# First MLP of an attention + MLP + MLP kernel: relu and square in the PSUM bank of h, the high half made by ScalarE

## The chip, the cores and the metric

One core of a Trainium2 chip runs the whole program. The metric is the device time of one execution in microseconds (us), lower is better. The engines are named as in the profile: PE (TensorE, matmuls), PEld (its weight loads), DVE (VectorE), ACT (ScalarE), POOL (GpSimd) and SP (SyncE, which issues the DMAs).

## What is computed

The reference, cut to what matters (4 batches, 8 heads, 576 queries of 64 columns; 2304 tokens, 512 columns, 2048 hidden columns):

```python
scores = scale * q @ k.T + (cum[:, None] - cum[None, :])   # cum: cumulated logs of f
attn = softmax(causal(scores));  x = attn @ v               # then (2304, 512)
h = x @ w_in;  r = maximum(h, 0);  g = s * (r * r) + b      # first MLP
x = g @ w_out
h = x @ w_in2; g = maximum(0.01 * h, h); out = g @ w_out2   # second MLP
```

The weights come as float64. Matmuls run on float32 values cut into a high and a low half; a product of two such numbers is three matmuls (high·high, high·low, low·high).

## The kernel before, in words

The tokens are cut into nine units of 256 queries. Units 0 to 7 are half a batch each; the last one, here called unit 8, has the 64 queries left over in every batch. While the first MLP of a unit runs, the attention of the next one is computed between its matmuls, on all engines.

The first MLP of a unit has 16 steps, i = 0 to 15, one for each 128 hidden columns. Step i has three parts. `mlp1_h` (L688) is 12 matmuls of 256 columns into a PSUM bank, h(i); there are two such banks (`ps_h`), and four from unit 7 on. `mlp1_g` makes g(i) = relu(h)² as a high and a low half in SBUF; the tile g has two buffers. `mlp1_o` (L733) is 12 matmuls that add g(i) times the weights to the unit's sums in the banks `ps_o`; the first two of them need only the high half, the third needs the low one. In the code o(i - 1) comes behind h(i) and g(i). The eviction of the sums at a unit's end is L747 (ACT) and L749 (DVE).

In `mlp1_g` of units 1 to 8 ACT reads the bank and writes relu to an SBUF tile `graw` (L711; two buffers), squares it there (L712), POOL copies it into g's high half, rounded (L713), and DVE subtracts that from `graw` to get the low half (L714). Unit 0 takes another path (L703, L704), which stays. In unit 7 two more columns of g are filled by POOL (L709, L710).

The attention of a head goes: scores on PE (L327), decay, mask and minimum on DVE (L337; POOL writes the mask into the tile `cumk`, L296, that a DMA loads), exp on ACT (L351), the two halves of the weights on ACT (L372) and DVE (L373), a transposing DMA into `p_t`, and the product with v on PE (L394); ACT and DVE add up the result (L413, L414, L428, L429). Queries and keys are split on POOL (L242, L243) and DVE (L244, L245).

Each block of float64 weights is turned into two halves by ACT (L102), DVE (L103, L104, L106), ACT (L111) and POOL (L112). The second matrix of the first MLP gets its halves in unit 1; the second MLP's blocks are made in unit 8 and in the first steps of the second MLP (L791 and L809 are its matmuls, L798 to L801 what lies between them).

The order on each engine is set when the program is built: a list scheduler places the instructions by priorities, by a cost table and by when buffers come free. On the chip each engine runs its own list strictly in that order, and waits at the first instruction whose input or buffer isn't ready.

Of the kernel before, what the change touches and what calls it, by code (L numbers as in the profile page):

```python
# [8 lines left out]
F32 = mybir.dt.float32  # L9
# [4 lines left out]
AF = mybir.ActivationFunctionType  # L14
ALU = mybir.AluOpType
AX = mybir.AxisListType

P = 128
NQ = 384
UN = 256  # L20
# [3 lines left out]
# Float32's bits under the sign are 8 times those of a float64's top word, less 896 of exponent:  # L24
# read as a float32 (whose exponent is 1/8 of that), the top word times this is that difference.
# [3 lines left out]
# A unit is 256 queries: all heads' attention, then the first MLP. The second unit of a batch attends  # L29
# for the batch's last 64 queries too, whose MLP comes with those of the other batches in a last unit.  # L30
# (batch, first query, queries, tiles of queries)
# [8 lines left out]
def attention_moe_moe_kernel(  # L40
# [42 lines left out]
    # They come as float64; the bits become float32 here, as hi + lo, both exact in float32r.  # L83
    # A block is a contraction tile's [128, 512]; raw and split blocks share the slots.
# [12 lines left out]
    def float_w(raw, out=None):  # L97
        """The bits of float32, in place of the top words or in a tile of their own."""
# [16 lines left out]
    class Weights:  # L115
        """Blocks 2i and 2i + 1 are of w_in and w_out. Those of w_out from `late` on stay float32 for a while."""
# [46 lines left out]
    heads = [(u, h) for u in range(1, NU - 1) for h in range(H)]  # L163
    # A job is a head's whole tiles of queries, the last first (the mask goes over the decays of keys
    # that earlier queries don't see), or, between two heads, both ones' half tile. A batch's first two
    # tiles go together, side by side.
# [9 lines left out]
    # A head's columns of queries: those of its half tile stand with zeros in place of the other head's.  # L176
# [12 lines left out]
    # A head's queries and keys: all of a tile's columns, or in turn one half of them.  # L189
# [6 lines left out]
    def load_heads():  # L196
        """Those whose place the heads that were split have left."""
        while n_qk[0] < len(heads) and n_qk[0] - 1 - (small(n_qk[0]) and small(n_qk[0] - 1)) < n_qk[1]:
            load_head(n_qk[0])
            n_qk[0] += 1  # L200
# [55 lines left out]
    def split_v(j, kend):  # L256
# [9 lines left out]
        # power of two at or under each column's largest magnitude, over PSCALE  # L266
# [19 lines left out]
    def st_mask(i):  # L286
        """The causal mask, over the decays."""
# [5 lines left out]
        for e in range(P // m):  # L293
            # (the second of two tiles has its keys behind the first's)
# [13 lines left out]
    def st_score(i):  # L308
# [7 lines left out]
        for r, t in enumerate(ts):  # L316
# [3 lines left out]
            for c, (k0, kw) in enumerate(parts):  # L320
# [13 lines left out]
                # Minus the scores, and their least. Of the decay, cum[query] - cum[key], the first term  # L334
                # is one to a row: the softmax is the same without it.
# [20 lines left out]
    def st_split(i):  # L356
        """Normalise; the weights as two halves, transposed by the DMA."""
# [73 lines left out]
    def last_x1():  # L431
        """The queries that the units of the batches left."""
# [43 lines left out]
    # The tensor engine has nothing else to do yet: it works in float32, adds the decay and the  # L476
    # mask, normalises and transposes.
# [20 lines left out]
    # The cumulated logs' hi and lo halves, on both halves of the partitions, then H columns with  # L498
    # -1/SCALE at a head's rows.
# [68 lines left out]
    def first_b(h):  # L568
# [11 lines left out]
        # by block of keys, then by the queries that see it  # L580
# [71 lines left out]
    def slot_target(u, i):  # L652
        """Slots of the attention that are to be emitted by then; not beyond the next unit but one's
        first pair of heads, whose x has to wait for a slot."""
        t0, t1 = (ends[v] + (AHEAD if heavy(v + 1) else LEAD) for v in (u, u + 1))
        t = t0 + ((i + 1) * (t1 - t0)) // NF
        if u + 2 < NU - 1:
            t = min(t, ends[u + 1] + (ends[u + 2] - ends[u + 1]) * 2 // H - 1)
        return t
# [4 lines left out]
    # The last unit with the attention behind it: there are banks for sums of their own.  # L664
# [32 lines left out]
    def mlp1_g(u, i, ps):  # L697
        # r^2 alone: s(r^2)W + (b 1)W is had from (r^2)W and, by two more columns in a unit, 1W.
        n = UN + 2 * (u == UB)
        if u == 0 and i >= W_FLOAT:  # L700
            # float32 products: the weights' halves come in the next unit
# [5 lines left out]
        raw = gp.tile([P, UN], F32, tag="raw", name="graw")  # L707
# [3 lines left out]
        nc.scalar.activation(raw, ps, AF.Relu)  # L711
        nc.scalar.activation(raw, raw, AF.Square)  # L712
        nc.gpsimd.tensor_scalar(g[:, 0, :UN], raw, 1.0, 0.0, ALU.mult, ALU.add)  # L713
        nc.vector.tensor_tensor(out=g[:, 1, :UN], in0=raw, in1=g[:, 0, :UN].bitcast(F32), op=ALU.subtract)  # L714
        return g[:, :, :n]

    def mlp1_po(u):
        """The unit's sums: two to a bank, a group of products together."""
# [231 lines left out]
```

## Time and profile before

| what | value |
|---|---|
| median of 3 runs | 1104.73 us (1100.14 to 1105.5) |
| span of the profiled execution | 1104.1 us |
| PE / PEld busy | 1004.9 / 884.5 us |
| DVE / ACT / POOL busy | 710.0 / 445.5 / 342.0 us |

The span runs from the first instruction of the profiled execution to its last. That execution's own time has no row apart from the span; the median lies 0.6 us above it. Busy times of the engines overlap. Units 1 to 6 take the stretch from about 143 to 599 us, unit 7 that to 642, unit 8 that to about 706, and the second MLP the rest.

### The profile page before, as it was taken

Reading aid. Unit: us, or ns where it says so; the run is one execution under the profiler, and the core shown is the slowest. Engines: PE = TensorE matmul, PEld = TensorE weight load, DVE = VectorE, ACT = ScalarE, POOL = GpSimd, SP = SyncE. Lnnn points to the kernel's source line nnn. Section 1 sums busy time; section 2 is a strip of 40 time slices with the busy share of each in tenths; the row PEclk is TensorE's granted clock in tenths of the full one; section 3 lists DMA queues with packets and bytes.
Section 4 is the critical chain, followed back from the end, with each engine's and each line's share of the span. In section 5 each row is a group of like instructions: output and inputs, shape, how many; then the busy total and the mean of one; then the engine's idle time right before and its main releaser. Section 6 shows DMA issues by size and latency. Waiting matters only on the chain.

```text
span 1104.1 us, 18869 instructions
## 1 busy us (share of the span) xinstructions
PE 1004.9 (91%) x6600; PEld 884.5 (80%) x6600; DVE 710.0 (64%) x1682; ACT 445.5 (40%) x1074; POOL 342.0 (31%) x591
## 2 busy tenths in 40 slices
PE   6876798889899988898989999899999999999998
PEld 4676687888888878787889999767888888888887
DVE  6788977776887877787765159998523533433343
ACT  4555566554555655555554235433101111111111
POOL 4344566644454444454431225433000000000000
PEclk9998989999999999999999999999999999999999
DMA  7388555469898998888874055450200010010010
GB/s 271 125 201 242 154 129 101 98 156 170 171 196 183 211 180 159 197 176 176 187 133 117 8 192 191 124 200 1 77 1 1 20 39 1 1 39 1 0 39 20
DMA packets 191791, 129.32 MB, mean 117 GB/s; under 512 B 137872, under 2 KB 167056, under 8 KB 191696
## 3 DMA queue, kind: packets, MB, share of 16 engines
q1 hardware_dynamic: 191696, 128.12, 48.2%
q8 instruction: 52, 0.85, 0.3%
q14 instruction: 43, 0.35, 0.1%
HBM read 86.58 MB, written 10.04 MB: 88 GB/s over the span
## 4 chain that ended last, share of the span: by engine, by line
PE 47%; DMA 17%; DVE 16%; issue 10%; POOL 6%; ACT 2%; SPq 1%; POOLq 0%; DVEq 0%; ACTq 0%
PE ps_o L809 16%; PE ps_h L791 15%; DMA p_t<-p_hl 7%; PE ps_o L733 6%; PE ps_h L688 6%; DMA cumk<-cumd 4%; DMA qk_raw<-in_qk 3%; DVE wt L104 2%; DVE tt L337 2%; POOL w L112 2%; DVE wt L106 1%; DVE p_hl L373 1%; DVE g L714 1%; POOL g L713 1%; PE ps_v L394 1%
## 5 line engine op out<-in xcount | busy, mean ns | idle before, releaser
L688 PE MATMUL ps_h<-x,w 128*128 128x256 f32 x1728 | 264.3, 288 | 13.2 <-POOL w L112 7.9
L733 PE MATMUL ps_o<-g,w 128*128 128x256 f32 (+1 forms) x1536 | 237.3, 292 | 16.5 <-POOL g L713 9.8
L688 PEld LDWEIGHTS ps_h<-x,w 128*128 128x128 f32 x1728 | 235.1, 194 | 17.1 <-POOL w L112 8.9
L733 PEld LDWEIGHTS ps_o<-g,w 128*128 128x128 f32 x1536 | 206.1, 193 | 27.2 <-POOL g L713 14.3
L809 PE MATMUL ps_o<-w,g 128*128 128x512 f32 x864 | 215.6, 396 | 5.2 <-DVE g L800 3.6
L791 PE MATMUL ps_h<-x,w 128*128 128x512 f32 (+1 forms) x960 | 211.0, 368 | 0.0
L809 PEld LDWEIGHTS ps_o<-w,g 128*128 128x128 f32 x864 | 159.7, 188 | 46.4 <-DVE g L800 6.3
L791 PEld LDWEIGHTS ps_h<-x,w 128*128 128x128 f32 x960 | 169.1, 188 | 32.1
L799 DVE TENSOR_TENSOR t<-ps_h,t 128x512 f32<-128x512 f32 (+1 forms) x80 | 50.8, 635 | 176.7 <-ACT t L798 176.4
L798 ACT ACTIVATE t<-ps_h 128x512 f32<-128x512 f32 (+1 forms) x80 | 44.3, 554 | 279.3 <-PE ps_h L791 279.3
L714 DVE TENSOR_TENSOR g<-graw,g 128x256 fp32r<-128x256 f32 x128 | 70.0, 549 | 66.0 <-POOL g L713 65.9
L351 ACT ACTIVATE tt<-tt,sm 128x512 f32<-128x512 f32 (+4 forms) x128 | 76.8, 600 | 88.3 <-DVE sm L337 79.3
L327 PE MATMUL ps_s<-k_st,q_st 128*128 128x288 f32 (+4 forms) x352 | 91.8, 335 | 20.3 <-DVE sm L337 10.1
L373 DVE SCALAR_TENSOR_TENSOR p_hl<-tt,sm,p_hl 128x512 f16<-128x512 f32 (+4 forms) x128 | 87.5, 692 | 22.5 <-ACT p_hl L372 21.4
L372 ACT ACTIVATE p_hl<-tt,sm 128x512 f16<-128x512 f32 (+4 forms) x128 | 73.5, 596 | 60.3 <-DMA p_t<-p_hl 46.5
L112 POOL TENSOR_TENSOR w<-wt,w 128x512 fp32r<-128x512 f32 x48 | 68.1, 1421 | 79.4 <-ACT w L111 77.8
L296 POOL TENSOR_SCALAR_AFFINE_SELECT cumk<-cumk 128x128 f32<-128x128 f32 (+2 forms) x120 | 46.9, 392 | 137.4 <-DMA cumk<-cumd 99.1
L394 PE MATMUL ps_v<-p_t,v_st 128*128 128x128 f16 (+1 forms) x912 | 60.5, 214 | 27.0 <-DMA p_t<-p_hl 23.8
L327 PEld LDWEIGHTS ps_s<-k_st,q_st 128*128 128x128 f32 x352 | 59.1, 194 | 26.6 <-DVE sm L337 15.1
L713 POOL TENSOR_SCALAR g<-graw 128x256 fp32r<-128x256 f32 x128 | 63.4, 497 | 50.7 <-ACT graw L712 41.1
L337 DVE CUSTOM_DVE_ANT_0 tt<-ps_s,cumk 128x512 f32<-128x512 f32 (+4 forms) x128 | 63.2, 497 | 23.5 <-POOL cumk L296 18.7
L394 PEld LDWEIGHTS <-v_st 128*128 128x128 f16 x912 | 46.8, 100 | 36.7 <-issue 15.8
(88 smaller groups left out, 1116.8 us busy)
## 6 DMA issues: line engine op xcount, KB each, us to landing
w_raw<-in_moe_w_in SPq DMA_DIRECT2D x32, 512.0 KB, 5.4
w_raw<-in_moe_w_out SPq DMA_DIRECT2D x32, 512.0 KB, 5.3
qk_raw<-in_qk SPq DMA_DIRECT2D x32, 480.0 KB, 4.5
cumk<-cumd SPq DMA_DIRECT2D x32, 256.0 KB, 4.3
qk_raw<-in_qk SPq DMA_DIRECT2D x24, 256.0 KB, 3.9
x1d<-x1o SPq DMA_DIRECT2D x36, 128.0 KB, 2.4
cumk<-cumd SPq DMA_DIRECT2D x32, 144.0 KB, 3.5
v_raw<-in_v SPq DMA_DIRECT2D x16, 288.0 KB, 4.2
```

Of the source, the lines that this page charges most:

```text
L112: nc.gpsimd.tensor_tensor(w[:, 1], x, w[:, 0].bitcast(F32), ALU.subtract)
L327: nc.tensor.matmul(o, q_st[j + e][:, q0 - u0 : q0 - u0 + P], k_st[j + e][:, a, k0 : k0 + kw], start=(e == 0 and a == 0), stop=(e == ne - 1 ...
L337: nc.vector.tensor_tensor_reduce(tt[:, at + k0 : at + k0 + kw], o, cumk[jb][:, at + k0 : at + k0 + kw], scale=-SCALE, scalar=3.0e38 if c = ...
L351: nc.scalar.activation(e, e, AF.Exp, bias=sm[:, r : r + 1], scale=-1.0, accum_out=sm[:, 2 + r : 3 + r])
L373: nc.vector.scalar_tensor_tensor(v[:, 1, :w], e, inv, v[:, 0, :w], ALU.mult, ALU.subtract)
L394: nc.tensor.matmul(av[:, at + e * m : at + (e + 1) * m], v_st[j + e][:, k].rearrange("p l d -> p (l d)"), pt[:, to + l * nk + k, e * m : ( ...
L688: nc.tensor.matmul(ps, wi[:, a, d * P : (d + 1) * P], x[:, c, d], start=(d == 0 and n == 0), stop=(d == ND - 1 and n == 2),)
L713: nc.gpsimd.tensor_scalar(g[:, 0, :UN], raw, 1.0, 0.0, ALU.mult, ALU.add)
L714: nc.vector.tensor_tensor(out=g[:, 1, :UN], in0=raw, in1=g[:, 0, :UN].bitcast(F32), op=ALU.subtract)
L733: nc.tensor.matmul(po[d], wo[:, a, d * P : (d + 1) * P], g[:, c], start=(first and n == 0), stop=(last and n == 2),)
L791: nc.tensor.matmul(ps[:, :n], wi[:, a, d * P : (d + 1) * P], x[:, e, d, :n], start=(d == 0 and k == 0), stop=(d == ND - 1 and k == 2),)
L809: nc.tensor.matmul(po[m], g[:, a, m * P : (m + 1) * P], wo[:, e, :], start=(i == 0 and k == 0), stop=(i == NF - 1 and k == 2),)
```

## The change

Relu and square of h now write back into the bank of h itself. ACT, in place of POOL, copies the bank into g's high half, and DVE subtracts from the bank. The tile `graw` is gone, and POOL has only the two extra columns of unit 7 left to do for g. The bank of h(i) is thus in use until the subtraction of step i has ended. Comments were also taken out of the file; as one line (the tile) is gone, lines behind it are one less in the changed kernel: relu, square, copy and subtraction are L710 to L713 there, and o(i) is L732.

```diff
         g = gp.tile([P, 2, UN + 2], F32R, tag="g", name="g", bufs=2)
-        raw = gp.tile([P, UN], F32, tag="raw", name="graw")
         if u == UB:
             nc.gpsimd.memset(g[:, 0, UN:].bitcast(F32), 1.0)
             nc.gpsimd.memset(g[:, 1, UN:].bitcast(F32), 0.0)
-        nc.scalar.activation(raw, ps, AF.Relu)
-        nc.scalar.activation(raw, raw, AF.Square)
-        nc.gpsimd.tensor_scalar(g[:, 0, :UN], raw, 1.0, 0.0, ALU.mult, ALU.add)
-        nc.vector.tensor_tensor(out=g[:, 1, :UN], in0=raw, in1=g[:, 0, :UN].bitcast(F32), op=ALU.subtract)
+        nc.scalar.activation(ps, ps, AF.Relu)
+        nc.scalar.activation(ps, ps, AF.Square)
+        nc.scalar.copy(g[:, 0, :UN], ps)
+        nc.vector.tensor_tensor(out=g[:, 1, :UN], in0=ps, in1=g[:, 0, :UN].bitcast(F32), op=ALU.subtract)
         return g[:, :, :n]
```

The scheduler places everything anew from unit 1 on. On PE, around the border of units 1 and 2, the list before reads as follows. It begins with o(14) of unit 1; then come h(1) and h(2) of unit 2, between scores (L327), and o(15) of unit 1 starts only behind them.

```order
L733 MATMUL ps_o<-g,w 128x256 x12
L688 MATMUL ps_h<-x,w 128x256 x8
L327 MATMUL ps_s<-k_st,q_st 128x128 x2
L688 MATMUL ps_h<-x,w 128x256 x4
L327 MATMUL ps_s<-k_st,q_st 128x128
L688 MATMUL ps_h<-x,w 128x256
L327 MATMUL ps_s<-k_st,q_st 128x128
L688 MATMUL ps_h<-x,w 128x256 x11
L733 MATMUL ps_o<-g,w 128x256 x4
```

The list of the change at the same place begins with the end of h(0) of unit 2; then come scores, o(15) of unit 1, and h(1) of unit 2 behind it.

```order
L688 MATMUL ps_h<-x,w 128x256 x4
L327 MATMUL ps_s<-k_st,q_st 128x288 x4
L327 MATMUL ps_s<-k_st,q_st 128x512
L732 MATMUL ps_o<-g,w 128x256 x2
L327 MATMUL ps_s<-k_st,q_st 128x512
L732 MATMUL ps_o<-g,w 128x256 x10
L688 MATMUL ps_h<-x,w 128x256 x5
```

What moved: h(i + 2) stood ahead of o(i) in 9 to 15 of the 16 steps in units 1 to 6, and does so in 0 to 5 of them now. In units 7 and 8, with four banks, it stands ahead in nearly all steps in both.

On ACT, in the first steps of unit 1, the list before reads as follows; each relu (L711) is followed closely by its square (L712), and nothing else of g is on this engine. L111 are the halves of the weights.

```order
L711 ACTIVATE graw<-ps_h 128x256
L111 CAST w<-w_raw 128x512
L712 ACTIVATE graw<-graw 128x256
L747 ACTIVATE x1o<-ps_o,sb 128x256
L351 ACTIVATE tt<-tt,sm 128x128
L372 ACTIVATE p_hl<-tt,sm 128x256
L372 ACTIVATE p_hl<-tt,sm 128x128
L413 COPY x_raw<-ps_v 64x256
```

The list of the change at that place, from the relu of step 2 to the one of step 3:

```order
L710 ACTIVATE ps_h<-ps_h 128x256
L372 ACTIVATE p_hl<-tt,sm 128x256
L372 ACTIVATE p_hl<-tt,sm 128x128
L711 ACTIVATE ps_h<-ps_h 128x256
L351 ACTIVATE tt,sm<-tt,sm 128x128
L111 CAST w<-w_raw 128x512
L413 COPY x_raw<-ps_v 64x256
L351 ACTIVATE tt,sm<-tt,sm 128x256
L372 ACTIVATE p_hl<-tt,sm 128x256
L372 ACTIVATE p_hl<-tt,sm 128x128
L710 ACTIVATE ps_h<-ps_h 128x256
```

What moved: the copies of steps 2 and 3 (L712 there) stand 32 and 24 rows behind their relus, with 28 and 21 instructions of other work between, and both banks of h are in use that long. Elsewhere in units 1 to 6 at most 6 instructions stand between, mostly 0 to 2. On PE, 95 matmuls stand from the end of h(2) of unit 1 to the start of its h(4), where 33 stood before; in the steps 2 and 3 of units 2 to 6 the list of the change has 61 to 85 there.

On POOL, at the end of the program, the list before goes through the copies of unit 8 (L713) between the low halves of the second MLP's weights (L112):

```order
L713 TENSOR_SCALAR g<-graw 128x256 x2
L112 TENSOR_TENSOR w<-wt,w 128x512
L713 TENSOR_SCALAR g<-graw 128x256
L112 TENSOR_TENSOR w<-wt,w 128x512
L713 TENSOR_SCALAR g<-graw 128x256
L112 TENSOR_TENSOR w<-wt,w 128x512
L713 TENSOR_SCALAR g<-graw 128x256 x2
L112 TENSOR_TENSOR w<-wt,w 128x512 x2
```

In the change the low halves of the weights follow each other behind the last of the extra columns of unit 7:

```order
L708 MEMSET g 128x2
L709 MEMSET g 128x2
L112 TENSOR_TENSOR w<-wt,w 128x512 x32
L945 UNCONDITIONAL_BRANCH
L945 ISA
```

What moved: no low half of a weight has a copy of g ahead of it any more.

## Rows read from the trace of the kernel before

**Rows 1.** Windows by stage: busy us of each engine, instructions, granted clock, DMA share.

```profile
143.00:218.00 75.00, 65.05 (x476) 61.10 (x476) 56.35 (x157) 46.06 (x129) 47.20 (x69) 0.91 0.53 116
218.00:599.00 381.00, 337.77 (x3021) 318.39 (x3021) 285.62 (x805) 208.40 (x519) 165.07 (x333) 0.99 0.83 171
599.00:642.00 43.00, 43.00 (x363) 43.00 (x363) 11.06 (x26) 13.63 (x35) 8.64 (x46) 1.00 0.12 38
642.00:706.00 64.00, 61.38 (x444) 56.91 (x443) 53.78 (x80) 32.73 (x70) 29.82 (x31) 1.00 0.52 170
706.00:757.00 51.00, 46.28 (x193) 34.70 (x191) 50.21 (x73) 20.92 (x35) 21.00 (x14) 1.00 0.50 169
757.00:1104.00 347.00, 342.48 (x1576) 282.45 (x1576) 138.75 (x252) 46.18 (x84) 4.48 (x3) 1.00 0.05 19
```

**Rows 2.** Waits of PE from 143 to 599 us: us, times, longest.

```profile
PE ps_v L394 <- DMA p_t<-p_hl: 20.3, 22, 2.2
PE ps_s L327 <- DVE sm L337: 9.1, 9, 2.4
PE ps_o L733 <- POOL g L713: 8.4, 9, 2.4
PE ps_o L733 <- DVE g L714: 4.0, 9, 0.9
```

**Rows 3.** Groups by line and shape: busy us, mean ns, idle us before, releasers.

```profile
L714 DVE TENSOR_TENSOR g<-graw,g 128x256 fp32r<-128x256 f32 x128 | 70.0, 549 | 66.0 <-POOL g L713 65.9
L713 POOL TENSOR_SCALAR g<-graw 128x256 fp32r<-128x256 f32 x128 | 63.4, 497 | 50.7 <-ACT graw L712 41.1 <-PE ps_v L394 3.0 <-issue 1.9
L712 ACT ACTIVATE graw<-graw 128x256 f32<-128x256 f32 x128 | 52.5, 413 | 2.4
L711 ACT ACTIVATE graw<-ps_h 128x256 f32<-128x256 f32 x128 | 47.9, 375 | 54.7 <-PE ps_h L688 34.1 <-DVE g L714 19.0 <-PE ps_s L327 0.5
```

**Rows 4.** Waits of DVE, then of POOL, from 143 to 599 us.

```profile
DVE g L714 <- POOL g L713: 26.1, 31, 2.3
DVE p_hl L373 <- ACT p_hl L372: 21.4, 26, 2.5
DVE tt L337 <- POOL cumk L296: 18.4, 17, 3.1
POOL cumk L296 <- DMA cumk<-cumd: 89.0, 49, 5.1
```

**Rows 5.** Single lines, all instructions: count, shortest, median and longest in ns.

```profile
L714 DVE TENSOR_TENSOR g<-graw,g x128: 398/426/1547, 150.0 to 696.9; 128x256 fp32r<-128x256 f32 x128
L799 DVE TENSOR_TENSOR t<-ps_h,t x80: 414/690/692, 696.3 to 1096.3; 128x512 f32<-128x512 f32 x64, 128x256 f32<-128x256 f32 x16
L801 DVE TENSOR_TENSOR g<-t,g x80: 424/692/1771, 699.1 to 1097.1; 128x512 fp32r<-128x512 f32 x64, 128x256 fp32r<-128x256 f32 x16
```

**Rows 6.** Groups by line and shape: subtraction in SBUF, maximum with one PSUM input.

```profile
L801 DVE TENSOR_TENSOR g<-t,g 128x256 fp32r<-128x256 f32 x16 | 6.8, 425 | 0.5
L799 DVE TENSOR_TENSOR t<-ps_h,t 128x256 f32<-128x256 f32 x16 | 6.8, 423 | 21.3 <-ACT t L798 21.0
```

**Rows 7.** Timeline in unit 8, DVE and POOL: start us, duration us, what.

```profile
677.41 1.48 POOL L112 TENSOR_TENSOR w<-wt,w 128x512 fp32r<-128x512 f32 x1 [2.80 <-ACT w L111]
677.78 1.66 DVE L106 SCALAR_TENSOR_TENSOR wt<-w_raw,wt 128x512 int32<-128x512 int32 x1
678.86 1.21 POOL L713 TENSOR_SCALAR g<-graw 128x256 fp32r<-128x256 f32 x2
679.74 2.04 DVE L714 TENSOR_TENSOR g<-graw,g 128x256 fp32r<-128x256 f32 x2 [0.30 <-POOL g L713]
680.18 1.32 POOL L112 TENSOR_TENSOR w<-wt,w 128x512 fp32r<-128x512 f32 x1
682.88 0.69 DVE L106 SCALAR_TENSOR_TENSOR wt<-w_raw,wt 128x512 int32<-128x512 int32 x1
686.64 2.05 DVE L714 TENSOR_TENSOR g<-graw,g 128x256 fp32r<-128x256 f32 x2 [0.30 <-POOL g L713]
```

**Rows 8.** Windows of line L714 alone: DVE busy us (instructions).

```profile
143.00:218.00 75.00, 11.94 (x15) 0.91 0.53 116
218.00:599.00 381.00, 39.86 (x81) 0.99 0.83 171
642.00:706.00 64.00, 11.41 (x16) 1.00 0.52 170
```

## Prediction

> **What bounds the kernel now.** I read the windows by stage first, to see which engine is short in which stage [rows 1]. From 757 us on, PE is busy 342.5 of 347 us. In unit 7, PE is busy without a gap: 363 matmuls in 43 us, 0.118 us for each. Neither stage can give anything. In units 1 to 6 (143 to 599 us) PE is busy 402.8 of 456 us; DVE has 342.0, ACT 254.5, POOL 212.3. No engine is full there: PE stands still for 53 us, because its list is strict and something that it needs comes late. In unit 8 and the start of the second MLP (642 to 757 us) DVE is busy 104.0 of 115 us, making the weights of the second MLP, and PE runs at less than the pace of unit 7: 444 matmuls in 64 us.
>
> So the kernel is bound by PE, and what can move is PE's 53 us of waits in units 1 to 6 and the DVE-bound stretch behind unit 7. The waits of PE say who is late [rows 2]: 20.3 us for transposed weights of the attention, 9.1 us for a score bank that DVE has not emptied, and 12.4 us for g: 8.4 for its high half from POOL and 4.0 for its low half from DVE. The change touches the 12.4 directly, and the 29.4 of the attention through the queues of DVE, ACT and POOL.
>
> **What goes away.** 128 copies on POOL at 0.497 us, 63.4 us of its time [rows 3]. They did harm beyond their time. POOL works in order, and it stood for 89.0 us in units 1 to 6 in front of the mask, until the DMA of cumk had landed [rows 4]; a copy of g queued behind that mask came late, and DVE, which is in order too, stood 26.1 us for it with attention work behind it.
>
> **The subtraction.** It took 0.549 us on average, but its median is 0.426 and its longest 1.547 [rows 3, 5]. The stretched ones lie beside POOL: at 679.74 two of them took 2.04 us while POOL made a weight's low half, and the next pair at 686.64 took 2.05 [rows 7]. The trace has no subtraction with one input in PSUM. The nearest row is L799, a two-input DVE operation of the same 128x256 with one input in PSUM, 0.423 us against 0.425 for the all-SBUF L801 [rows 6]; and of 80 such none took over 0.692 at 512 columns, where L801 went up to 1.771 [rows 5]. I take 0.43, that is 0.12 less, 15.2 us of DVE in all: 10.5 in units 1 to 6 (11.94 + 39.86 = 51.8 [rows 8], less 96 x 0.43 = 41.3) and 4.5 in unit 8 (11.41 less 6.9). The bounds are 0.40, the shortest now, and 0.55, where nothing is gained.
>
> [...]
>
> **What ACT gets.** A copy out of PSUM like L711, 0.375 us, 128 times: 48 us. Relu and square now write PSUM, which no ACT row shows. The square from SBUF to SBUF takes 0.413, the relu from PSUM to SBUF 0.375 [rows 3]. Upper bound: the two stay as they are, and ACT gets 48 us. Lower bound: writing PSUM saves as much as reading it does, 0.04 for each of the two, and one more 0.04 as the square now reads it: 33 us. I take 0.375 for all three, plus 43 us, some 32 of it in units 1 to 6. ACT goes there from 254.5 to about 287 of 456 us, 56 to 63%.
>
> **The sum, on PE's path.**
>
> (a) The waits for g, 12.4 us. The work from h to both halves takes 0.375 + 0.413 + 0.497 + 0.549 = 1.83 us now, and 3 x 0.375 + 0.43 = 1.56 afterwards, with one engine fewer in between, and that the one whose list stops for DMAs. But the list of the change also gives it less time: h(i + 2) now mostly stands behind o(i), so that less work covers the chain. I take half, minus 6 us; bounds 0 and minus 12.4.
>
> (b) The attention's 29.4 us. DVE loses its 26.1 us of standing for POOL and 10.5 us of work; POOL's list is free of g, so that masks, for which DVE stood 18.4 us [rows 4], come sooner. Much of this is slack, since a transpose's transfer time stays. I take a quarter, minus 7; bounds 0 and half, minus 15.
>
> (c) Unit 8. DVE gets 4.5 us back where it is the bound. But POOL's low halves still fall on DVE's work: at 677.41 one stretched L106 to 1.66, where another took 0.69 [rows 7]. If the subtraction is no longer stretched, its neighbour may be. I take minus 2; bounds 0 and minus 4.5.
>
> (d) ACT's 32 us lie in front of the attention's exp and weights. DVE already stands 21.4 us for the high half of the weights [rows 4]; 13% more work on ACT makes that some 3 us longer. I put plus 3 on PE; bounds 0 and plus 6.
>
> (e) The bank. With graw gone, a bank of h is free only after the subtraction. In the steady steps that costs nothing: o(i) stands ahead of h(i + 2) and needs the same subtraction, so there is no wait of its own. At the start of a unit o is late (the sums of the unit before must be evicted), and then relu could run two steps further into graw; now h stops when two g and two banks are full. In unit 1 the copies of steps 2 and 3 stand 28 and 21 instructions behind: at ACT's mean of 0.357 us (46.06 us for 129 [rows 1]) that is 10 and 7.5 us. PE has 95 matmuls of its own in that time, about 11 us at unit 7's pace and less at the attention's shorter ones, so little of it shows. I take 2 us for unit 1 and 2 for the other five; bounds 0 and 3 for each unit, 18. What is queued behind the waiting h on PE is the attention's next scores, for which DVE and ACT would wait.
>
> Together: -6 - 7 - 2 + 3 + 4 = -8 us. The profiled execution has a span of 1104.1 us, the median is 1104.7, so I work from either: about 1097 us, 0.7% less. A measurement of this kernel, whose three runs differ by 0.5%, can tell some 0.5%, 5.5 us, from no change.
>
> **The rivals.**
>
> *More of the waits go* (chance 0.14). Were the order of the lists better served all over, (a) would give 9, (b) 11, (c) 3, with (d) as above and nothing for (e): minus 20, 1085 us. For it: DVE's 26.1 us in front of g and POOL's 89.0 in front of the masks. Against it: the largest of PE's waits is for a transposing DMA, which stays.
>
> *No change* (0.27). Half of (a) and (b) come true, minus 6.5; (c) minus 2; ACT and the bank take 3 + 4 back: minus 1.5, 1103 us. For it: the engines other than PE are not full in units 1 to 6, so that relieving two of them and loading a third may move only slack.
>
> *The bank stops PE at the units' starts* (0.23), the one on the other side. Two h fewer ahead are 24 matmuls, at 0.118 us 2.8 us for each of six starts, 17 us. With half of (a) and (b), and (c) and (d) as above, that is plus 11.5, 1116 us. For it: the order on ACT in unit 1 and the loss of run-ahead in all six lists. Against it: PE's list at those places was filled with attention. It decides from 1.8 us at each start on: then the 11 us exceed the gains left, 5.5, by as much as can be told. [...]
>
> That the change does less than it says is not a rival: the lists show POOL without g.
>
> **How the numbers follow.** My forecast, minus 6 to minus 15 us, has 0.36. With the larger gain, faster holds 0.50; no change 0.27; slower 0.23. One in ten on either side leaves out what lies beyond the larger gain's 1085 below, and the upper part of the bank's case above: 1086 to 1114. The forecast alone reaches from 1090 to 1099.
>
> **What would show it.** Right: no wait of DVE for POOL in g; the subtraction at 0.42 to 0.43 with none above 0.5; POOL near 280 us busy, ACT near 489, DVE under 700; PE's waits for g under 7 us in units 1 to 6; unit 8 and the start of the second MLP 1 to 4 us shorter. (d) is wrong if DVE stands much longer than 25 us for L372. (e) is wrong if PE stands for the subtraction ahead of L688, or for scores at units' starts, more than 10 us in all; unit 1 would show it first, as a stretch well over its 75 us. The prediction fails above all if the new lists place the attention worse, which no row of the old trace can show: then PE's waits for p_t and for score banks grow past 29 us.

## The result, and the profile after

The changed kernel took 1114.87 us in the median of 4 runs (1111.99 to 1118.84); the kernel before took 1102.74 beside it. The ratio is 1.0119, with a 95% interval from 1.0086 to 1.0153: slower by 1.2%, 13 us by the ratio and 12 by the medians, and just above the upper end of the predicted range.

The page of the changed kernel, busy times and granted clock:

```profile
span 1113.1 us, 18783 instructions
PE 1017.5 (91%) x6600; PEld 895.1 (80%) x6600; DVE 693.7 (62%) x1682; ACT 481.7 (43%) x1202; POOL 288.1 (26%) x463
PEclk9988888899999999999999999999999999999999
```

PE executes the same 6600 matmuls and is busy 12.6 us longer, while the span grew by 9.0: over the whole span PE stands still for less time than before (95.6 us against 99.2; in units 1 to 6 for more, as a table below shows), and its matmuls take longer (154.2 ns of busy time for each, against 152.3). The other engines did what the change says: DVE is down by 16.3 us, POOL by 53.9, ACT up by 36.2. The groups of the four lines, answering to [rows 3] (busy us, mean ns, idle before):

```profile
L713 DVE TENSOR_TENSOR g<-ps_h,g 128x256 fp32r<-128x256 f32 x128 | 53.4, 418 | 44.6 <-ACT g L712 43.7
L712 ACT CAST g<-ps_h 128x256 fp32r<-128x256 f32 x128 | 46.7, 366 | 8.0 <-PE ps_o L732 4.8 <-DVE x L780 0.4
L711 ACT ACTIVATE ps_h<-ps_h 128x256 f32<-128x256 f32 x128 | 47.0, 367 | 2.8
L710 ACT ACTIVATE ps_h<-ps_h 128x256 f32<-128x256 f32 x128 | 47.0, 367 | 46.2 <-PE ps_h L688 45.7
```

The subtraction of all 128 steps (shortest, median, longest in ns), answering to [rows 5]:

```profile
L713 DVE TENSOR_TENSOR g<-ps_h,g x128: 399/420/429, 149.9 to 702.9; 128x256 fp32r<-128x256 f32 x128
```

So each operation came out as costed, and none of that shows in the time. For the stages I take the first relu of each unit as its start. The first two units of the kernel before, by windows (us from and to, length, then busy us and count of PE, PEld, DVE, ACT, POOL, granted clock, DMA share, GB/s):

```profile
142.60:217.90 75.30, 65.35 (x479) 61.38 (x477) 56.65 (x157) 46.34 (x130) 47.35 (x70) 0.91 0.53 115
217.90:291.30 73.40, 65.11 (x550) 60.84 (x549) 54.78 (x156) 38.02 (x99) 31.47 (x65) 1.00 0.76 158
```

The changed kernel, units 1, 2 and 4:

```profile
141.30:230.90 89.60, 71.10 (x517) 65.93 (x516) 63.85 (x196) 56.30 (x165) 46.93 (x67) 0.89 0.50 119
230.90:311.20 80.30, 69.76 (x545) 64.55 (x544) 53.87 (x148) 41.19 (x108) 23.09 (x46) 0.91 0.72 149
...
390.30:467.30 77.00, 70.09 (x631) 65.82 (x632) 58.33 (x177) 48.77 (x126) 28.43 (x56) 0.98 0.90 185
```

Unit 1 grew by 14.3 us and unit 2 by 6.9; later ones gave part of that back (unit 4 took 85.4 us before). The extra in unit 1 lies in its first four steps: from the first relu to the fifth it is 21.2 us before and 35.4 afterwards. This is PE in that stretch (start us, us, then what; in brackets the idle time ahead and who ended it):

```profile
150.36 1.67 PE L688 MATMUL ps_h<-x,w 128*128 128x256 f32 x12 [1.59 <-DVE g L713]
152.04 0.92 PE L732 MATMUL ps_o<-g,w 128*128 128x256 f32 x6
153.69 1.60 PE L688 MATMUL ps_h<-x,w 128*128 128x256 f32 x12
155.14 0.63 PE L732 MATMUL ps_o<-g,w 128*128 128x256 f32 x4
157.96 0.84 PE L327 MATMUL ps_s<-k_st,q_st 128*128 128x128 f32 x4 [2.19 <-DVE sm L337]
...
161.90 1.01 PE L327 MATMUL ps_s<-k_st,q_st 128*128 128x128 f32 x3 [2.75 <-DVE sm L337]
166.26 0.69 PE L327 MATMUL ps_s<-k_st,q_st 128*128 128x128 f32 x2 [1.53 <-DVE sm L337]
168.66 0.80 PE L394 MATMUL ps_v<-p_t,v_st 128*128 128x128 f16 x6 [1.71 <-DVE x_raw L414]
169.29 2.93 PE L732 MATMUL ps_o<-g,w 128*128 128x256 f32 x12
...
175.12 1.57 PE L688 MATMUL ps_h<-x,w 128*128 128x256 f32 x12
```

And ACT's and DVE's rows of the same stretch that hold the banks: the relus of steps 2 and 3, the two copies, and the last eviction of unit 0's sums:

```profile
152.40 0.37 ACT L710 ACTIVATE ps_h<-ps_h 128x256 f32<-128x256 f32 x1
159.14 0.36 ACT L710 ACTIVATE ps_h<-ps_h 128x256 f32<-128x256 f32 x1
172.76 0.37 ACT L712 CAST g<-ps_h 128x256 fp32r<-128x256 f32 x1
173.58 0.38 ACT L712 CAST g<-ps_h 128x256 fp32r<-128x256 f32 x1
...
168.75 0.48 DVE L748 TENSOR_SCALAR x1o<-ps_o,sb 128x256 f32<-128x256 f32 x1
```

Read it backwards. h(4) starts at 175.12, when its bank has been copied (172.76) and subtracted. That copy needs a buffer of g; both were held by steps 0 and 1, whose products with the second half of the columns run at 169.29. (ACT comes to the copy a little later than that needs: ahead of it, it stands 2.07 us for a transfer of p_t, until 171.93.) Those products need the second sums' bank, which DVE evicts at 168.75 (the first one was evicted by 151). From 155.8 to 169.3 PE's list holds nothing but attention, and most of its pieces wait for DVE: PE is busy for 4.9 of these 13.5 us, and for 11.8 of the 19.7 between 157 and 176.7. With `graw` the same four steps had room to go on.

PE's waits in units 1 to 6 (us, times, longest), answering to [rows 2]:

```profile
PE ps_v L394 <- DMA p_t<-p_hl: 14.6, 17, 2.7
PE ps_s L327 <- DVE sm L337: 11.6, 9, 2.7
PE ps_o L732 <- DVE g L713: 9.0, 13, 2.4
PE ps_o L732 <- ACT g L712: 7.7, 9, 2.5
PE ps_v L394 <- DVE x_raw L414: 5.7, 5, 1.7
```

Those for g rose from 12.4 to 16.7 us. DVE and POOL in the same stretch, answering to [rows 4]:

```profile
DVE p_hl L373 <- ACT p_hl L372: 47.5, 40, 3.9
DVE tt L337 <- POOL cumk L296: 18.1, 21, 3.0
...
POOL cumk L296 <- DMA cumk<-cumd: 108.7, 53, 10.7
```

DVE's 26.1 us of standing for POOL's copy are gone, and as much has come back in front of L373 (21.4 to 47.5). The masks came no sooner (18.4 to 18.1): POOL, with less to do, stood longer for the transfer that it masks (89.0 to 108.7).

### The profile page after: what moved, and what is told of

It is laid out like the page before. It is cut to its first block, busy times and chain, and to the rows that moved or that the text cites. A ratio compares the mean times of both kernels' runs of the same rounds, so it can differ in the third digit from the quotient of the medians.

```text
span 1113.1 us, 18783 instructions
## 1 busy us (share of the span) xinstructions
PE 1017.5 (91%) x6600; PEld 895.1 (80%) x6600; DVE 693.7 (62%) x1682; ACT 481.7 (43%) x1202; POOL 288.1 (26%) x463
## 4 chain that ended last, share of the span: by engine, by line
PE 50%; DMA 21%; DVE 13%; issue 7%; POOL 4%; ACT 4%; SPq 1%; POOLq 0%; DVEq 0%; ACTq 0%
PE ps_o L808 15%; PE ps_h L790 14%; DMA p_t<-p_hl 11%; PE ps_o L732 7%; PE ps_h L688 7%; DMA cumk<-cumd 5%; POOL w L112 2%; DVE wt L104 2%; PE ps_v L394 2%; DVE p_hl L373 2%; PE ps_s L327 2%; DMA qk_raw<-in_qk 2%; DVE tt L337 1%; ACT p_hl L372 1%; DVE wt L106 1%
## 5 line engine op out<-in xcount | busy, mean ns | idle before, releaser
L688 PE MATMUL ps_h<-x,w 128*128 128x256 f32 x1728 | 252.1, 292 | 10.1 <-POOL w L112 7.3
L732 PE MATMUL ps_o<-g,w 128*128 128x256 f32 (+1 forms) x1536 | 238.5, 296 | 21.1 <-DVE g L713 9.7
L688 PEld LDWEIGHTS ps_h<-x,w 128*128 128x128 f32 x1728 | 229.6, 198 | 12.1 <-POOL w L112 8.5
L732 PEld LDWEIGHTS ps_o<-g,w 128*128 128x128 f32 x1536 | 208.7, 197 | 33.6 <-DVE g L713 15.5
L790 PEld LDWEIGHTS ps_h<-x,w 128*128 128x128 f32 x960 | 169.3, 188 | 32.4
L373 DVE SCALAR_TENSOR_TENSOR p_hl<-tt,sm,p_hl 128x512 f16<-128x512 f32 (+4 forms) x128 | 83.6, 663 | 47.8 <-ACT p_hl L372 47.5
L372 ACT ACTIVATE p_hl<-tt,sm 128x512 f16<-128x512 f32 (+4 forms) x128 | 73.6, 597 | 82.0 <-DMA p_t<-p_hl 72.2
L327 PE MATMUL ps_s<-k_st,q_st 128*128 128x288 f32 (+4 forms) x352 | 83.6, 340 | 18.9 <-DVE sm L337 11.6
L296 POOL TENSOR_SCALAR_AFFINE_SELECT cumk<-cumk 128x128 f32<-128x128 f32 (+2 forms) x120 | 51.6, 433 | 183.3 <-DMA cumk<-cumd 124.0
L112 POOL TENSOR_TENSOR w<-wt,w 128x512 fp32r<-128x512 f32 x48 | 72.1, 1501 | 88.2 <-ACT w L111 83.1
L394 PE MATMUL ps_v<-p_t,v_st 128*128 128x128 f16 (+1 forms) x912 | 64.4, 215 | 23.8 <-DMA p_t<-p_hl 16.9
L713 DVE TENSOR_TENSOR g<-ps_h,g 128x256 fp32r<-128x256 f32 x128 | 53.4, 418 | 44.6 <-ACT g L712 43.7
L327 PEld LDWEIGHTS ps_s<-k_st,q_st 128*128 128x128 f32 x352 | 57.9, 200 | 25.8 <-DVE sm L337 15.6
L337 DVE CUSTOM_DVE_ANT_0 tt<-ps_s,cumk 128x512 f32<-128x512 f32 (+4 forms) x128 | 63.3, 497 | 23.5 <-POOL cumk L296 18.1
L710 ACT ACTIVATE ps_h<-ps_h 128x256 f32<-128x256 f32 x128 | 47.0, 367 | 46.2 <-PE ps_h L688 45.7
```

The lines of the kernel that those rows point to most:

```text
L112: nc.gpsimd.tensor_tensor(w[:, 1], x, w[:, 0].bitcast(F32), ALU.subtract)
L327: nc.tensor.matmul(o, q_st[j + e][:, q0 - u0 : q0 - u0 + P], k_st[j + e][:, a, k0 : k0 + kw], start=(e == 0 and a == 0), stop=(e == ne - 1 ...
L337: nc.vector.tensor_tensor_reduce(tt[:, at + k0 : at + k0 + kw], o, cumk[jb][:, at + k0 : at + k0 + kw], scale=-SCALE, scalar=3.0e38 if c = ...
L372: nc.scalar.mul(v[:, 0, :w], e, inv)
L373: nc.vector.scalar_tensor_tensor(v[:, 1, :w], e, inv, v[:, 0, :w], ALU.mult, ALU.subtract)
L394: nc.tensor.matmul(av[:, at + e * m : at + (e + 1) * m], v_st[j + e][:, k].rearrange("p l d -> p (l d)"), pt[:, to + l * nk + k, e * m : ( ...
```

## The theories and the experiments

Theory 1: the bank of h, held until the subtraction, takes two steps of run-ahead away at a unit's start, above all in unit 1. Theory 2: ScalarE's added work delays the attention. Theory 3: any edit makes the scheduler place all lists anew, and another placing alone may cost a per cent. All ratios are to the kernel before, run in turns with it on the same chip.

### Four kernels that part the bank from the copy

`e1_sbuf_act` keeps the tile `graw` and moves only the copy to ScalarE:

```diff
-        nc.scalar.activation(ps, ps, AF.Relu)
-        nc.scalar.activation(ps, ps, AF.Square)
-        nc.scalar.copy(g[:, 0, :UN], ps)
-        nc.vector.tensor_tensor(out=g[:, 1, :UN], in0=ps, ...
+        raw = gp.tile([P, UN], F32, tag="raw", name="graw")
+        nc.scalar.activation(raw, ps, AF.Relu)
+        nc.scalar.activation(raw, raw, AF.Square)
+        nc.scalar.copy(g[:, 0, :UN], raw)
+        nc.vector.tensor_tensor(out=g[:, 1, :UN], in0=raw, ...
```

> The change with graw kept in SBUF: relu frees the bank of h, ScalarE still makes the high half, VectorE still subtracts, GpSimd has nothing for g. If the held bank costs the time (theory 1), unit 1 takes 75 to 78 us again instead of 89.6, PE's windows there show a granted clock near 1, and the ratio to the kernel before is 0.990 to 1.000, since POOL's relief then comes without its price. If ScalarE's added work does it (theory 2), ScalarE is as loaded as in the change or a little more, unit 1 stays near 90 us and the ratio near 1.012. If any other order of the lists would move the time by a per cent (theory 3), the units lose and gain in other places than unit 1, and the ratio may stand anywhere from 0.99 to 1.01.

`e2_g3` is the change with a third buffer of g (unit 0's tile of the same name, not shown, gets it too):

```diff
-        g = gp.tile([P, 2, UN + 2], F32R, tag="g", name="g", bufs=2)
+        g = gp.tile([P, 2, UN + 2], F32R, tag="g", name="g", bufs=3)
```

> The change with three buffers of g instead of two, one step of h more ahead, the bank still held until the subtraction. Theory 1: the third g gives back one of the two steps that were lost, so that unit 1 takes 76 to 84 us, and the ratio to the kernel before is 0.992 to 1.004. Theory 2: ScalarE does the same work, so 1.012. Theory 3: any of 0.99 to 1.01, without unit 1 as the place.

`e3_unit1_sbuf` is the change with `graw` in unit 1 alone:

```diff
-        nc.scalar.activation(ps, ps, AF.Relu)
+        if u == 1:
+            raw = gp.tile([P, UN], F32, tag="raw", name="graw")
+            nc.scalar.activation(raw, ps, AF.Relu)
+            ps = raw
+        else:
+            nc.scalar.activation(ps, ps, AF.Relu)
```

> The change, but in unit 1 alone relu, square, copy and subtraction go through an SBUF tile; the other units keep the bank. Theory 1 with the loss in unit 1: that unit takes about 75 us, the units behind it keep what they had, and the ratio to the kernel before is 0.998 to 1.002. If the loss comes from the held bank in all units' starts alike, the ratio is 1.007 to 1.010. Theory 2: no change from 1.012.

`e4_act_load` is the kernel before with a copy on ScalarE that nothing reads:

```diff
+        spare = gp.tile([P, UN], F32, tag="spare", name="spare", bufs=1)
+        nc.scalar.copy(spare, raw)
```

> The kernel before with one more copy of ScalarE in each step of the first MLP, from graw to a spare tile, that nothing reads: some 48 us more on ScalarE, GpSimd and VectorE as before, banks as before. Theory 1: the units keep their times within 2 us each, the ratio is 0.998 to 1.005. Theory 2: ScalarE's load alone makes it slower by the change's 12 us, 1.008 to 1.015.

Measured, with the change first:

| kernel | median us (runs) | ratio [95%] | first to fifth relu of unit 1 | unit 1 |
|---|---|---|---|---|
| the change | 1114.87 (4) | 1.0119 [1.0086, 1.0153] | 35.4 us | 89.6 us |
| e1_sbuf_act | 1100.52 (10) | 0.9972 [0.9942, 1.0002] | 21.0 | 72.3 |
| e2_g3 | 1104.63 (10) | 0.9999 [0.9980, 1.0017] | 21.0 | 74.6 |
| e3_unit1_sbuf | 1103.92 (10) | 1.0007 [0.9984, 1.0029] | 22.4 | 70.2 |
| e4_act_load | 1107.76 (10) | 1.0037 [1.0014, 1.0060] | 20.8 | 75.0 |

Three ways to give back the run-ahead each take away the whole loss, with the copy still on ScalarE. All three ratios are as theory 1 expected; the times of unit 1 are a little shorter than it said. Theory 2 falls as the main cause: `e4_act_load` has even more ScalarE work (487.6 us on the page against 481.7) and is slower by 0.37%, 4 us, not 1.2%. (Not all of its units kept their times within 2 us, as theory 1 had it: unit 3 grew by 4.8 and unit 4 shrank by 4.4.) `e2_g3` holds the banks until the subtraction, as the change does; one more g is enough. `e3_unit1_sbuf` points at unit 1, since the five other units kept the held bank. Its windows of units 1 and 2 warn against adding up, though:

```profile
142.00:212.20 70.20, 62.45 (x481) 58.55 (x479) 51.83 (x156) 48.74 (x142) 38.40 (x53) 0.95 0.58 122
212.20:296.60 84.40, 71.24 (x580) 65.71 (x580) 61.20 (x187) 48.95 (x133) 33.52 (x60) 0.98 0.76 164
```

Unit 1 is 5 us shorter than before and unit 2 is 11 us longer: attention that one unit doesn't take in is left to the next.

### Necessary, sufficient, and a control

`e5_x1o4` is the change with four buffers of x1o, the tile that an eviction writes and a DMA stores, so that an eviction need not wait for the store of an earlier one:

```diff
-            o = mp.tile([P, UN], F32, tag="x1o", name="x1o", bufs=2)
+            o = mp.tile([P, UN], F32, tag="x1o", name="x1o", bufs=4)
```

> The change with four buffers of x1o instead of two: all four evictions of a unit's sums can be done without waiting for the store of an earlier one; g and the banks of h as in the change. Theory 1 in its closer form (the banks of h are held because g is, g is held because the first sums of the new unit wait for the late second pair of evictions): the second pair lands by about 157 us instead of 162.5 and 168.8, the banks come free and unit 1 takes 76 to 82 us instead of 89.6; ratio to the kernel before 0.998 to 1.006. Rival: the evictions are only late because PE's list is, and unit 1 stays near 88 us; ratio 1.010 to 1.014.

`e6_unit1_psum` is the kernel before with the change in unit 1 alone:

```diff
+        if u == 1:
+            raw = ps
         nc.scalar.activation(raw, ps, AF.Relu)
         nc.scalar.activation(raw, raw, AF.Square)
-        nc.gpsimd.tensor_scalar(g[:, 0, :UN], raw, 1.0, 0.0, ALU.mult, ALU.add)
+        if u == 1:
+            nc.scalar.copy(g[:, 0, :UN], raw)
+        else:
+            nc.gpsimd.tensor_scalar(g[:, 0, :UN], raw, 1.0, 0.0, ALU.mult, ALU.add)
```

> The kernel before, but in unit 1 alone relu and square stay in the bank of h, ScalarE copies the high half and VectorE subtracts from the bank; GpSimd makes g in the other units. Theory 1, unit 1 is where it is lost: unit 1 takes 88 to 91 us as in the change, the ratio to the kernel before is 1.007 to 1.013. If the loss needs the bank in the other units too, unit 1 may still be long but the later ones give it back, and the ratio is 0.998 to 1.005.

`e7_sbuf_x1o3` is `e1_sbuf_act`, and `e9_before_x1o3` the kernel before, both with `bufs=3` for x1o.

> The first experiment (graw in SBUF, copy on ScalarE) with three buffers of x1o. If evictions held up by a store cost PE at every unit's start also where the bank is free early, this gains some 0.5 us for each of six starts: ratio 0.990 to 0.996, and it would be a version that beats both. If run-ahead into graw already covers them, the same ratio as the first experiment, 0.994 to 1.000.

> The kernel before with three buffers of x1o and nothing else: a control for the others, and a measure of what another order of the lists does by itself, since unit 1's start keeps its order and the later units' lists are placed anew. Theory 1: within 0.4% of the kernel before. Theory 3 (any new order may cost a per cent): beyond 0.5% on either side.

| kernel | median us (runs) | ratio [95%] | first to fifth relu of unit 1 | unit 1 |
|---|---|---|---|---|
| e5_x1o4 | 1104.67 (10) | 1.0019 [0.9998, 1.0041] | 22.8 us | 82.6 us |
| e6_unit1_psum | 1113.62 (6) | 1.0089 [1.0059, 1.0120] | 35.8 | 89.6 |
| e7_sbuf_x1o3 | 1099.88 (10) | 0.9971 [0.9955, 0.9987] | 21.4 | 74.6 |
| e9_before_x1o3 | 1114.05 (4) | 1.0103 [1.0075, 1.0131] | 20.7 | 78.2 |

`e5_x1o4` bears out the chain that was read backwards above; its rival, evictions that are late only because PE's list is, expected unit 1 near 88 us. These are the evictions of unit 0's sums in it (ACT and DVE: first and last start):

```profile
L746 ACT ACTIVATE x1o<-ps_o,sb x2: 463/466/468, 149.8 to 152.1; 128x256 f32<-128x256 f32 x2
L748 DVE TENSOR_SCALAR x1o<-ps_o,sb x2: 473/480/486, 150.9 to 152.6; 128x256 f32<-128x256 f32 x2
```

In the change, where the third and fourth eviction need the buffers of the first two:

```profile
L746 ACT ACTIVATE x1o<-ps_o,sb x2: 467/470/474, 149.5 to 162.5; 128x256 f32<-128x256 f32 x2
L748 DVE TENSOR_SCALAR x1o<-ps_o,sb x2: 474/479/484, 150.6 to 168.8; 128x256 f32<-128x256 f32 x2
```

In the kernel before, with two buffers as well:

```profile
L747 ACT ACTIVATE x1o<-ps_o,sb x2: 458/466/473, 150.9 to 155.9; 128x256 f32<-128x256 f32 x2
L749 DVE TENSOR_SCALAR x1o<-ps_o,sb x2: 474/479/484, 152.2 to 156.4; 128x256 f32<-128x256 f32 x2
```

In the change SyncE issues the stores of the first two evictions at 157.5 and 164.5 us, behind transfers of the attention. The first lands at 159.7, and the third eviction comes 2.8 us later, in its place on ACT's list; the second lands at 168.7, and the fourth eviction starts at once. With the last one at 152.6 instead of 168.8, the four steps take 22.8 us, and 1.0% of the time is back, with another list too: 68 matmuls stand between h(2) and h(4) there. `e6_unit1_psum` shows the converse: unit 1's stall alone, in otherwise the old kernel, with the same list there, makes it 0.9% slower. But it did not just add 14 us. Counted from unit 1's first relu in both, it stands 14.6 us behind the kernel before at the fifth relu, up to 18 in unit 2, 3 to 9 in unit 3, up to 14 in unit 5 and 9.7 at the end: attention that was taken in early is saved later, and the later lists, placed anew as well, lose again. `e7_sbuf_x1o3` gained nothing over `e1_sbuf_act` (0.9971 and 0.9972): of the two readings put down for it, that run-ahead into `graw` already covers a late eviction is the one that fits.

`e9_before_x1o3` is the surprise, and theory 1 alone had not expected it. One more buffer, no more work, no held bank, and it is 1.0% slower. Unit 3 is where most of it is lost (the kernel before first, then this one); unit 4 gave 5.8 us of that back, and 4.2 us more were lost from unit 7 on:

```profile
291.30:366.00 74.70, 68.39 (x602) 63.85 (x600) 60.26 (x173) 43.28 (x109) 36.47 (x72) 0.98 0.94 190
292.50:378.10 85.60, 72.80 (x645) 68.53 (x644) 62.30 (x178) 44.80 (x112) 41.69 (x77) 0.96 0.87 183
```

with these waits of PE in it, of which the kernel before had 2.3 us for the first:

```profile
PE ps_v L394 <- DMA p_t<-p_hl: 8.5, 10, 2.2
PE ps_s L327 <- POOL q_st L243: 1.6, 1, 1.6
```

So theory 3 holds too: an edit's own effect and that of the new placing come together. The last four kernels measure pairs.

### Pairs with the same second edit

`e10_after_x1o3` is the change with three buffers of x1o. The three others exchange the engines of the evictions, in the kernel before, in the change and in `e1_sbuf_act`:

```diff
-            if d % 2 == 0:
+            if d % 2 == 1:
                 nc.scalar.mul(o, po[d][:, :UN], sb[:, 0:1])
             else:
                 nc.vector.tensor_scalar(o, po[d][:, :UN], sb[:, 0:1], None, ALU.mult)
```

> The change with three buffers of x1o, the edit that made the kernel before 1.0% slower. Its list holds the banks at unit 1's start nearly as long as the change's (81 matmuls of other work between two h, where the change has 95 and 89). Theory 1, as narrowed: unit 1 takes 84 to 90 us, ratio to the kernel before 1.007 to 1.014. Theory 3, the placing of the lists decides and not the bank: the ratio may stand anywhere from 0.995 to 1.014.

> The kernel before with the two engines of the evictions of the first MLP's sums exchanged (VectorE takes even parts, ScalarE odd ones), an edit that changes no work and no buffer but places the lists anew. Theory 1: 0.996 to 1.004. Theory 3: up to 1% off, as with three buffers of x1o.

> The change with the same exchange of the evictions' engines. Its list at unit 1's start still holds the banks (87 and 85 matmuls of other work). Theory 1: unit 1 takes 84 to 90 us, its ratio to the kernel before 1.007 to 1.014, and above that of the exchange on the kernel before by 0.7 to 1.4%. Theory 3: no such steady distance between the two.

> The first experiment (graw in SBUF, copy on ScalarE) with the same exchange. Theory 1: no held bank, so within 0.4% of the exchange on the kernel before and 0.994 to 1.001 of the kernel before. Theory 3: up to 1% off.

| kernel | median us (runs) | ratio [95%] | first to fifth relu of unit 1 | unit 1 |
|---|---|---|---|---|
| e10_after_x1o3 | 1106.36 (10) | 1.0014 [0.9995, 1.0033] | 29.4 us | 82.2 us |
| e11_before_swap | 1101.67 (10) | 0.9963 [0.9943, 0.9982] | 19.8 | 75.0 |
| e12_after_swap | 1113.11 (4) | 1.0078 [1.0051, 1.0105] | 32.2 | 84.9 |
| e13_sbuf_swap | 1105.94 (10) | 1.0022 [1.0001, 1.0043] | 20.8 | 74.5 |

Set side by side by their second edit, the ratios are:

| second edit | POOL copies from graw (before) | ACT copies from graw | ACT copies from the bank (change) | bank held: third less second |
|---|---|---|---|---|
| none | 1 | 0.9972 | 1.0119 | +1.47% |
| x1o with 3 buffers | 1.0103 | 0.9971 | 1.0014 | +0.43% |
| evictions exchanged | 0.9963 | 1.0022 | 1.0078 | +0.56% |

The kernel with the held bank is the slower one in all three pairs, by 0.4 to 1.5%. In each of them the four first steps of unit 1 are longer, by 14.4, 8.0 and 11.4 us. The copy's move from POOL to ACT goes from -1.3 to +0.6%: its sign isn't settled by these. That spread also says how far to trust the last column: the two kernels of a pair differ in the placing of their lists as well, which here is worth as much as the differences, so the column's sign is better founded than its size. Theory 1 as narrowed got `e12_after_swap` right and `e10_after_x1o3` wrong (1.0014 for 1.007 to 1.014, unit 1 82.2 us for 84 to 90), and `e13_sbuf_swap` lies 0.6% above `e11_before_swap` where 0.4% was the bound.

Over all fourteen kernels: the ten whose four first steps of unit 1 take under 23 us have ratios from 0.9963 to 1.0103, all but `e9_before_x1o3` under 1.004; the four with 29 to 36 us have 1.0014 to 1.0119, all but `e10_after_x1o3` over 1.007. The whole change is slower by 1.2% in two rows and faster by 0.9% in the third (1.0014 / 1.0103 = 0.991), because there it is the kernel before that lost 1.0% by the second edit.

The profiled executions (nine of them below) also say what the time consists of. For units 1 to 6, I cut the stretch into slices of 4 us and added up PE's idle time, and PE's busy time multiplied by what the granted clock lacks to 1 (a slice of 4.00 us busy at 0.58 counts as 1.68), an estimate of what the lower clock cost. Four such slices of the changed kernel, the first two in unit 1's stall, at a granted clock of 0.50, the last two in unit 2:

```profile
161.00:165.00 4.00, 2.35 (x10) 1.68 (x10) 3.12 (x10) 3.02 (x11) 1.65 (x2) 0.50 0.39 94
165.00:169.00 4.00, 1.03 (x6) 0.97 (x7) 3.01 (x10) 2.98 (x11) 2.08 (x3) 0.50 0.55 184
237.00:241.00 4.00, 1.70 (x10) 1.35 (x10) 3.90 (x10) 2.80 (x9) 1.64 (x2) 0.99 0.22 38
241.00:245.00 4.00, 4.00 (x23) 3.48 (x23) 3.61 (x16) 2.63 (x8) 0.40 (x2) 0.58 0.57 147
```

| kernel | idle us | lost to the lower clock us | sum | unit 1's start to the end, us |
|---|---|---|---|---|
| before | 53.2 | 11.1 | 64.3 | 961.5 |
| the change | 56.6 | 19.1 | 75.7 | 971.8 |
| e6_unit1_psum | 59.0 | 14.9 | 73.9 | 971.2 |
| e9_before_x1o3 | 58.2 | 13.0 | 71.2 | 971.5 |
| e12_after_swap | 57.9 | 12.0 | 69.9 | 969.5 |
| e4_act_load | 57.4 | 6.2 | 63.6 | 964.8 |
| e1_sbuf_act | 53.6 | 12.9 | 66.5 | 961.8 |
| e3_unit1_sbuf | 53.6 | 8.9 | 62.5 | 961.0 |
| e7_sbuf_x1o3 | 50.6 | 11.7 | 62.3 | 956.8 |

The slow kernels are those with the larger sums (the five kernels left out have 62.0 to 65.2). In this execution of the change the idle time is larger by only 3.4 us and the estimated loss to the clock by 8.0: PE stood for short whiles, and behind the one before 241 us the granted clock was 0.58 over 4 us in which PE had full work. That is an account of one execution of each kernel, and the clock's share of it is not shown to be the kernel's own. The granted clock over the whole program ran from 0.959 to 0.986 in 77 executions of the kernel before, and those at the higher clock were not the shorter ones (a median of 1104.9 us for the 41 above 0.975, 1102.6 for the 36 others); the change took 1114.85 us at 0.965, in the execution read here, and 1114.89 at 0.977. No experiment kept the clock up through the stall.

## Why the prediction was wrong

**The step that failed is (e), the bank**, and in it one sentence: that PE's 95 matmuls of its own, "about 11 us at unit 7's pace and less at the attention's shorter ones", would fill the time of the late copies. The matmuls were there, and the copies were late, by about twice the estimate (20.4 and 14.4 us behind their relus, for 10 and 7.5). But the time was taken from PE's pace in unit 7, where PE has no gap [rows 1]. In unit 1 half of these matmuls (46 of the 94 in the trace) are attention, most pieces of which wait for DVE: for its minimum, itself behind a mask whose DMA POOL waits for, or for its sum of the products with v. From the end of h(2) at 152.0 to h(4) at 175.1 they took 23 us. The sign named for it came, unit 1 at 89.6 us for 75. The term of 2 us for unit 1 measured 14.2 in the four steps; for the kernel, the term of 4 us measured 16, 5 and 6 us in the three pairs (1.47, 0.43 and 0.56% of 1103), with the placing in it, the first within its upper bound of 18.

The term is not the whole of the miss. From the forecast, minus 8, to the change, plus 13, are 21 us. In the pair without a second edit 12 of them are the bank (16 us for the 4 put down). The other 9 are gains that did not come: (a) to (d) were to give 12 together, and `e1_sbuf_act`, which has them without the held bank, gave 3 (0.28%, with an interval from nothing to 0.6%). The terms that failed there are (b) and (c), below.

Of what the bank waits for, the prediction named the late eviction of the sums and the two g and two banks that fill. But it took its price from ACT's list; what sets the time is a ring of full buffers: bank, g, sums, x1o, and a store issued late. It would have been found by asking, for each buffer that becomes scarce, what frees the one behind it.

The rival on the other side, the bank stopping PE at the units' starts, named the right mechanism and nearly the right time, 1116 us for 1114.9. Its place was too wide, so that the time is partly luck: it spread 17 us over six starts, and one start carried it, as far as `e3_unit1_sbuf` and `e6_unit1_psum` show. The tile graw, which frees the bank after one operation, was worth 0.4 to 1.5% in the three pairs, with the placing in it.

**(a) The waits for g.** Expected: from 12.4 to 6 us. In `e1_sbuf_act`, where only the engine of the copy changed, it is just that; its waits of PE in units 1 to 6:

```profile
PE ps_v L394 <- DMA p_t<-p_hl: 23.6, 20, 4.1
PE ps_s L327 <- POOL q_st L243: 7.6, 6, 2.4
PE ps_s L327 <- DVE sm L337: 5.2, 8, 1.4
PE ps_o L733 <- DVE g L714: 4.1, 8, 1.3
...
PE ps_o L733 <- ACT g L713: 1.9, 5, 0.5
```

In the change they are 16.7: with h(i + 2) behind o(i), little work covers the shorter chain. The prediction named this and took half for it; it took more than all.

**(b) The attention's waits.** Expected: minus 7. The same rows show that nothing came: the waits of PE for p_t and for score banks are 28.8 us there (29.4 before), and the one for POOL's q_st grew from 1.2 to 7.6. PE's idle time in units 1 to 6 is 53.6 us against 53.2. In the change the two are 26.2, not past the 29 named as the sign of attention placed worse, but the wait for DVE's sum (L414) rose from 1.1 to 5.7. DVE's relief turned into a longer stand for ACT's half of the weights (21.4 to 44.5 us in `e1_sbuf_act`), ahead of which ACT itself stood longer for the transfers of p_t (46.5 to 65.6 over the whole program); POOL's turned into a longer stand for cumk's (99.1 to 112.8, likewise). Here two engines that are not full did not hasten a chain whose next link is a transfer.

**(c) Unit 8.** Expected: minus 2. From unit 7's start to the end it is 504.9 us before and 506.9 in the change, 502.4 in `e1_sbuf_act`. Nothing that can be told.

**(d) ACT.** Expected: plus 3 from plus 43 us of work. The work was plus 36.2, and `e4_act_load`, with plus 42.1 (487.6 less 445.5), took 4 us more (1.5 to 6.6 by its interval). That agrees, as far as a new placing lets one say. That DVE stands 47.5 us for L372, over the 25 named as the sign against (d), is not ACT's load alone: in `e4_act_load` it is 27.6, in `e1_sbuf_act` 44.5, so that it comes where the copy leaves POOL.

**The subtraction.** 0.418 us for the 0.43 assumed, none longer than 0.429. That one input lies in PSUM made no difference that shows: from SBUF the shortest and the median are 397 and 420 ns, from PSUM 399 and 420. For comparison the line in `e1_sbuf_act`, both inputs in SBUF, POOL without g:

```profile
L714 DVE TENSOR_TENSOR g<-graw,g x128: 397/420/1514, 149.8 to 693.4; 128x256 fp32r<-128x256 f32 x128
```

**What stays open.** How much of the 13 us would be left if the later lists could be kept: the stall of unit 1 is shown, added alone and taken away in four ways, but what of it reaches the end was between 5 and 16 us, with the placing. And the share of the clock is read from one execution of each kernel, and the clocks of the other executions speak against a fixed share.

A version that beats both: `e7_sbuf_x1o3`, 0.9971 [0.9955, 0.9987]; `e11_before_swap`, which leaves g as it was, is as good at 0.9963 [0.9943, 0.9982]. Neither gain is larger than what placing alone does here.

## What to carry to other kernels

To keep an intermediate in PSUM lengthens the hold of a bank by every engine that still reads it (in step 2 of unit 1 the copy came 20.4 us behind the relu): before you drop a staging tile, write down the ring of buffers at the place where run-ahead is needed, each with what frees it, and time the work that is to fill the gap by its own waits in that place, not by the engine's pace elsewhere. Relief of engines that are not full was worth here what their chain's next link let through; that was a DMA, and it came to nothing that could be told (53.6 us of PE's idle time in units 1 to 6 of `e1_sbuf_act`, 53.2 before). And where a scheduler places everything anew, one comparison holds the edit's effect and the placing's: pair both kernels with a second, idle edit before you believe a difference of a per cent.

## What the runs showed of the hardware

A subtraction on DVE with one input in PSUM was never stretched by POOL's work beside it (longest 429 ns of 128, 49 of which ran beside a POOL instruction), while the same one from SBUF was, up to 1514 and 1547 ns, the first of them in `e1_sbuf_act`, where POOL had nothing to do with g: all 40 over 460 ns in the kernel before ran beside a POOL instruction. ACT's relu and square took 367 ns each from PSUM to PSUM, against 375 from PSUM to SBUF and 413 from SBUF to SBUF, and its copy 366 from PSUM and 400 from SBUF. And work behind a stall of PE was slower too at one place of the change: behind 4 us in which PE was busy for 1.70, the next 4.00 us of full work, from 241 us on, went at a granted clock of 0.58, and the six matmuls of the sums in them took 416 ns on average, against 295 in unit 4.
